# A spectral layer's row folds, made for four rows at once on one engine, with half of them made ahead of the layer

## The chip, the cores and the metric

The kernel runs on one core of one Trainium2 chip. A core has a matrix engine (TensorE; PE in the profile, with its weight loads as PEld), VectorE (DVE), ScalarE (ACT), GpSimd (POOL) and SyncE (SP), whose queue issues nearly every DMA of this kernel. All share one on-chip memory, SBUF; matmuls write to PSUM banks, from which ACT or DVE copy. The metric is the time of one execution on the device in microseconds (us); lower is better. Everything is float32 unless said otherwise.

## The reference

Four layers follow each other on a 2048 x 512 array: a spectral layer A, a state-space convolution B, A again with the same weights, B again with the same kernel. Cut to what matters:

```python
x = A_x                                            # (1, 2048, 512)
x = x + A(layernorm(x), w_r, w_i)                  # A: irfft2(rfft2(x) * (w_r + 1j * w_i))
x = x + B(layernorm(x), ...)                       # B: convolution along the rows, kernel K, plus x * D
x = x + A(layernorm(x), w_r, w_i)
x = x + B(layernorm(x), ...)

def B(u):
    C = (C_real + 1j * C_imag) * dt
    A = -exp(log_A_real) + 1j * A_imag
    K = 2 * einsum("dn,dnl->dl", C, exp(A * dt * l)).real
    return irfft(rfft(u, 4096) * rfft(K, 4096))[:2048] + u * D
```

Each layer norm is over the 512 columns of a row, without scale or shift.

## The kernel before

The 2048 rows are held as 128 partitions times 16 rows (`n2`, 0 to 15); a partition holds 16 rows of 512 columns. Every Fourier transform is a matmul with a cosine and sine matrix.

**Layer A** (`layer_a`) has three lists of steps. `spread(n2)`, L411 to L456, folds one row: with the 512 columns as four blocks of 128 (0 to 3), it makes f = blocks 0 and 1 plus blocks 2 and 3 (L443) and the difference (L444), and from these the four symmetric parts xf that a real transform needs. Part 0 is the sum of f's two blocks with the mean taken off (L447), part 1 their difference (L448), parts 2 and 3 the difference and the sum of one difference block and the other one read backwards (L449, L450), and L451 copies the one column that has no partner. In the second A layer L443, L444, L447 and L448 run on DVE and L449 to L451 on POOL (`SPL2 = 'vvggg'`). L435 on ACT scales the 128 x 128 transform matrix of that row by one over the row's deviation, four matmuls (L454) multiply the parts by it, and two ACT copies (L456) put the result into the array z. The rows are normed in groups of 2, 2, 4, 4, 4 (`GA2`) by `layer_norm_stats`, a chain of small operations: L337, L342, the square root L349 on ACT, L350, L353, L354, L355, L357, on DVE but for the root. `middle(t)` transforms the columns (`forward`, L465 to L469), multiplies by the weights, which come by DMA into `wt` tiles (L481; L483 on POOL mends two columns when they have landed; L495 is the product on DVE), and transforms back; `end(t)` folds back, adds the row and norms it.

**Layer B** (`layer_b`) goes through four blocks of 128 columns, 0 to 3. For a block `weigh` multiplies by the kernel's transform (matmul L313, products L914, sums L926 and L927 on DVE and POOL), and `back` transforms back: `units` (matmul L939, ACT copy L940) and `rows` (matmul L947, four rows at a time), in which L956 on DVE adds the layer's input `xs`, loaded by DMA (L952), and writes the sum into `h` (tile `za`), and L961 gathers the statistics for the next norm. So after block 3's four `rows` steps the second A layer has its input. The statistics of a row are whole only then; the columns of blocks 0 to 2 are final earlier.

**The order around the change.** The recording order is written out by hand (`interleave` merges lists of steps evenly). A scheduler then sets each engine's order from the recorded program by its own estimate of time, and every engine works through its own list in that order; an instruction whose wait is not over holds up what is behind it on its engine, and a DMA whose wait is not over holds up those behind it on SP. At the end of the first B layer, L1001 to L1007 record the four `rows` steps of block 3 and then all of the second A layer's `spread` steps.

**Room.** Tiles of one tag share slots in turn, and a new user waits for the readers of the old one. `t` holds B's row matrix T (2 MB), `t2` B's way back (2 MB). The transform matrix `ta` (1 MB, loaded in two pieces, L302) takes the room of `t2` and so waits for the last L947; the matrix for the way back, `in_tat`, takes it after that. Small tiles `w` share 7 slots: xs, f, xf, the scaled matrix, and the `wt` loads of the middle stage, which are tag `w` there too.

Of the kernel before, what the change touches and what calls it, by code (L numbers as in the profile page):

```python
# [19 lines left out]
RL = 4  # L20
# [12 lines left out]
LAGE = 3  # L33
# [8 lines left out]
GA2 = '22444'  # L42
# [5 lines left out]
SPL2 = 'vvggg'  # L48
# [5 lines left out]
TS2 = 'a'  # L54
# [189 lines left out]
class Net:  # L244
# [71 lines left out]
    def layer_norm_stats(self, rows, newton=False, sums=None, times=None, nr=None):  # L316
# [35 lines left out]
        for k in range(steps):  # L352
            nc.vector.scalar_tensor_tensor(t, r, -0.5, r, op0=ALU.mult, op1=ALU.mult)  # L353
            nc.vector.tensor_mul(t, t, e)  # L354
            nc.vector.scalar_tensor_tensor(nr[:, 1] if k == steps - 1 else r, t, 1.5, r, op0=ALU.add, op1=ALU.mult)  # L355
        if times is not None:
            nc.vector.tensor_scalar_mul(nr[:, 0], m, sign * times)  # L357
        else:
            nc.vector.scalar_tensor_tensor(nr[:, 0], m, -sign, nr[:, 1], op0=ALU.mult, op1=ALU.mult)
        return nr  # L360
# [18 lines left out]
    def layer_a(self, w, x=None, src=None, dst=None):  # L379
# [5 lines left out]
        spl, ya, zc, ye, we, ts = (SPL, YA, ZC, YE, WE, TS) if x is None else (SPL2, YA2, ZC2, YE2, WE2, TS2)  # L385
# [21 lines left out]
        starts = np.cumsum([0, *map(int, GA if x is None else GA2)]).tolist()  # L407
# [3 lines left out]
        def spread(n2):  # L411

            if n2 in starts:
                norm["from"] = n2
                G = starts[starts.index(n2) + 1] - n2
                norm["rows"] = [row(k_, here[k_ // 8][:, k_ % 8]) if x is None else x[:, k_] for k_ in range(n2, n2 + G)]
                if x is None and not S1:
                    norm["nr"] = self.layer_norm_stats(norm["rows"], newton=NW[0] == "1", times=-4.0)
                elif x is None:
                    norm["f"] = [self.sb("w", [2, 256]) for _ in range(G)]  # L420
                    sums = self.sb("lsum", [G], 2)
                    for k_, f in enumerate(norm["f"]):
                        r = norm["rows"][k_]
                        self.add_up(f[:, 0], r[:, 0:256], r[:, 256:512], sums[:, k_:k_ + 1])
                    norm["nr"] = self.layer_norm_stats(norm["rows"], sums=sums, times=-4.0)
                else:
                    norm["nr"] = self.layer_norm_stats([self.stats[:, n2 + k_] for k_ in range(G)], newton=NW[1] == "1", times=-4.0)
# [6 lines left out]
            if ts == "a":  # L434
                nc.scalar.activation(t, k["T"][:, n2], ACT.Copy, scale=r)  # L435
            else:
                adders[ts].tensor_scalar(t, k["T"][:, n2], r, None, op0=ALU.mult)
            x01 = split(rows[i], "abc", [2, 2, 128])
            if x is None and S1:
# [6 lines left out]
            e = [adders[c] for c in spl]  # L446
# [8 lines left out]
            for i in range(2):  # L455
                nc.scalar.copy(ZA[i][:, :, :, n2, :], p[:, :, 64 * i:64 * i + 64].rearrange("p b (q c) -> p b q c", c=4))  # L456

# [126 lines left out]
        def end(t):  # L584
            if t < 16:
                fold(t)
            if 0 <= t - LAGE < 16:
                rows_back(t - LAGE)

        return ([partial(spread, t) for t in range(16)], [partial(middle, t) for t in range(18)],  # L590
                [partial(end, t) for t in range(16 + LAGE)])
# [303 lines left out]
    def layer_b(self, kf, T, out, x=None, src=None, first=None, more=(), fill=(), switch=(), kept=None, after=None):  # L895
# [79 lines left out]
        for i, (blk, _, _, pairs) in enumerate(chain):  # L975
# [8 lines left out]
            parts = [fill[i][a:b] for a, b in zip(n, n[1:])]  # L984
            then = chain[i + 1] if i + 1 < len(chain) else (None, [], [])
# [15 lines left out]
        if after:  # L1001
            then = after()
            n = [0] * RL + list(range(0, len(then), 16 // len(last)))
            for i, f in enumerate(last):
                f()
                interleave(then[n[i]:n[i + 1]])
            last = then[n[len(last)]:]  # L1007
        interleave(last)
# [27 lines left out]
def net_kernel(ctx, tc, x, w, ends, kin, log_dt, d_skip, out, **cst):  # L1036
# [14 lines left out]
    with ExitStack() as outer:  # L1051
        with ExitStack() as early:
# [28 lines left out]
            def after():  # L1081
                wide.close()
                net.tags["wb"] = net.tags["w"]
                outer.enter_context(net.phase("x", side="right", x=(32768, 1)))
# [6 lines left out]
            wide = ExitStack()  # L1091
# [26 lines left out]
        h = net.h  # L1118
        for s in A[1:]:
# [36 lines left out]
```

## Time and profile before

| what | us |
|---|---|
| median of 3 runs (lowest, highest) | 825.46 (825.22, 829.8) |
| the profiled execution's own time | 827.06 |
| its span, first to last instruction | 825.3 |
| first B layer's last weigh sum on POOL ends | 552.65 |
| last matmuls of its way back (L947) | 558.49 to 565.90 |
| DVE: from the first L956 of block 3 to the last L448 | 560.58 to 595.96 |
| middle stage: first L465, first L495 | 598.04, 601.68 |

Engine busy time over the span is PE 82%, DVE 80%, ACT 52%, POOL 51%. These are averages over stages with different limits; what the change is worth is read from the stretch between 520 and 602 us.

### The profile page before, as it was taken

To read this page: it belongs to the slowest core of one execution; us is meant where nothing else is said; L and a number is where in the kernel's file an instruction comes from. 1 tells how busy PE (TensorE), PEld (TensorE's weight loads), DVE (VectorE), ACT (ScalarE), POOL (GpSimd) and SP (SyncE) were. 2 spreads that over 40 slices of the span, in tenths; PEclk is the share of its full clock that TensorE was granted. 3 is DMA by queue.
4 is the path that set the end of the run, shared out by engine and by line. 5 is a ranking of instruction groups with operands and counts; after the bars stand their busy time and mean duration, and the time that the engine had idled before them with its cause. 6 is when DMAs were issued, how large, how long until landed. Compare 5 with 4: busy or idle time off the path is not lost. (4 is left out here: it accounts for less than half of the span.)

```text
span 825.3 us, 13571 instructions
## 1 busy us (share of the span) xinstructions
PE 678.4 (82%) x4544; PEld 483.2 (59%) x4544; DVE 657.6 (80%) x1333; ACT 432.8 (52%) x911; POOL 419.9 (51%) x642
## 2 busy tenths in 40 slices
PE   3347889887779878799679989967799897999996
PEld 3336656664445535566356757656577673568766
DVE  7999649798998869887897868558877796977692
ACT  3525779655567855667656634213566436333212
POOL 3675876745624024822275425072855571755661
PEclk9657989999979979999989999989999999999999
DMA  8201633253566231451316557301133015323411
GB/s 323 91 1 31 148 89 107 47 136 109 140 214 178 99 44 49 90 174 35 72 33 135 185 101 209 115 1 52 54 89 89 29 27 178 102 80 100 128 49 55
DMA packets 144188, 82.24 MB, mean 100 GB/s; under 512 B 78228, under 2 KB 123928, under 8 KB 143352
## 3 DMA queue, kind: packets, MB, share of 16 engines
q1 hardware_dynamic: 143864, 80.87, 34.6%
q0 software_dynamic: 256, 0.52, 0.4%
q8 instruction: 36, 0.59, 0.3%
q14 instruction: 32, 0.26, 0.1%
HBM read 56.86 MB, written 25.03 MB: 99 GB/s over the span
## 5 line engine op out<-in xcount | busy, mean ns | idle before, releaser
L927 POOL TENSOR_TENSOR u<-wb,wb 64x512 f32<-64x512 f32 x64 | 91.9, 1436 | 121.8 <-DVE wb L914 107.1
L313 PE MATMUL p<-z,mb 128*64 128x512 f32 (+1 forms) x480 | 102.5, 542 | 6.9 <-DVE wb L914 4.5
L454 PE MATMUL p<-w,w 128*128 128x128 f32 x256 | 53.2, 369 | 51.4 <-DVE w L447 35.3
L605 ACT COPY z<-p 128x512 f32<-128x512 f32 x96 | 57.9, 615 | 70.4 <-PE p L604 60.8
L914 DVE TENSOR_TENSOR wb<-p,kk 128x512 f32<-128x512 f32 x128 | 81.3, 679 | 13.8 <-PE p L313 10.4
L827 PE MATMUL pv<-qp 128*64 128x128 f32 x1024 | 78.8, 295 | 10.4 <-DVE qp L816 8.3
L827 PEld LDWEIGHTS pv<-qp 128*64 128x64 f32 x1024 | 62.4, 146 | 40.0 <-issue 13.2
L816 DVE TENSOR_TENSOR qp<-qp,mag 128x1024 f32<-128x1024 f32 x64 | 84.9, 1331 | 0.8
L814 DVE SCALAR_TENSOR_TENSOR qp<-qp,mag 128x256 f32<-128x256 f32 x128 | 66.2, 530 | 18.7 <-ACT qp L757 18.3
L454 PEld LDWEIGHTS p<-w,w 128*128 128x128 f32 x256 | 45.1, 262 | 59.1 <-issue 25.0
L939 PE MATMUL p<-mb,u 128*128 128x128 f32 x512 | 69.0, 290 | 8.4 <-POOL u L926 6.9
L939 PEld LDWEIGHTS p<-mb,u 128*128 128x128 f32 x512 | 65.2, 203 | 16.8 <-POOL u L926 9.9
L611 DVE STREAM_TRANSPOSE z<-z 128x512 f32<-128x512 f32 x96 | 58.4, 674 | 16.5 <-ACT z L605 16.5
L940 ACT COPY u<-p 128x512 f32<-128x512 f32 x64 | 37.4, 588 | 55.7 <-PE p L939 55.6
L495 DVE TENSOR_TENSOR w<-wt,p 128x514 f32<-128x514 f32 x64 | 42.6, 687 | 30.1 <-PE p L313 20.7
L604 PE MATMUL p<-t,w 128*128 128x256 f32 x256 | 64.9, 387 | 1.0 <-POOL w L1025 0.8
L947 PEld LDWEIGHTS p<-u,t 128*128 128x128 f32 x512 | 59.1, 192 | 11.0 <-issue 5.1
L947 PE MATMUL p<-u,t 128*128 128x128 f32 x512 | 62.8, 279 | 1.4 <-ACT u L940 1.4
L313 PEld LDWEIGHTS p<-z,mb 128*64 128x64 f32 x480 | 34.0, 141 | 46.2 <-issue 24.0
L926 POOL TENSOR_TENSOR u<-wb,wb 64x512 f32<-64x512 f32 x32 | 44.6, 1394 | 22.4 <-PE p L939 17.9
L795 DVE TENSOR_SCALAR kw<-pk 128x512 bf16<-128x512 f32 x64 | 43.2, 682 | 13.4 <-PE pk L793 13.3
L604 PEld LDWEIGHTS p<-t,w 128*128 128x128 f32 x256 | 45.5, 190 | 13.6 <-issue 5.9
(189 smaller groups left out, 1552.6 us busy)
## 6 DMA issues: line engine op xcount, KB each, us to landing
wt<-in_w SPq DMA_DIRECT2D x32, 257.0 KB
w<-h SPq DMA_DIRECT2D x32, 256.0 KB
kf<-kk SPq DMA_DIRECT2D x32, 256.0 KB
kk<-kf SPq DMA_DIRECT2D x32, 256.0 KB
u<-in_x SPq DMA_DIRECT2D x16, 256.0 KB
hr<-in_x SPq DMA_DIRECT2D x16, 256.0 KB
kt<-stage SPq DMA_DIRECT2D x32, 128.0 KB
h<-hr SPq DMA_DIRECT2D x16, 256.0 KB
```

The costliest lines, as they stand in the source:

```text
L313: last = self.nc.tensor.matmul(out, weights, data, start=True, stop=True, skip_group_check=True).ins
L454: nc.tensor.matmul(p[:, b], xf[:, b], t, start=True, stop=True)
L604: nc.tensor.matmul(p[:, i], src(n2 + i), T[:, n2 + i], start=True, stop=True)
L605: nc.scalar.copy(Z[:, :, n2:n2 + 2, :].rearrange("p u n r -> p n u r"), p.rearrange("p n (u r) -> p n u r", r=2))
L611: nc.vector.transpose(tiles["zt"][:, u:u + 16].rearrange("p u d -> p (u d)"), tiles["z"][:, u:u + 16].rearrange("p u n r -> p (u n r)"))
L814: nc.vector.scalar_tensor_tensor(QP[:, c, 0], QP[:, c, 1, :, ::-1], -1.0 if c else 1.0, m[:, 0], op0=ALU.mult, op1=ALU.mult)
L816: nc.vector.tensor_mul(t, t, mag[:, None, 1:3, 256 * j:256 * j + 256].to_broadcast([128, 2, 2, 256]))
L827: nc.tensor.matmul(p[64 * t:64 * t + 64, g], QP[:, c, 2, d:d + 2].rearrange("p s a -> p (s a)"), QP[:, c, 0:2, d:d + 2].rearrange("p k s b ...
L914: nc.vector.tensor_mul(split(m[c, pl], "du", [16, 32]), by_channel(p), split(k[c], "du", [16, 32]))
L927: e[1].tensor_add(y[64:128], v[0, 1], v[1, 0])
L939: nc.tensor.matmul(p[:, i], Y[:, d + i], MBT, start=True, stop=True)
L947: nc.tensor.matmul(p[:, i], TBT[:, n0 + i, r], V[:, n0 + i, r].rearrange("p q d -> p (q d)"), start=r == 0, stop=r == 1)
```

## The change

Only the second A layer's first stage and its neighbours are touched.

- The even blocks' folds, block 0 plus block 2 and block 0 minus block 2, are made in eight DVE operations of four rows each while block 3 is still to be done (block 2's columns are final by then). They are kept in a tile `even` of 16,384 bytes per partition, in T's room, whose last reader in this layer was the forward transform of block 3.
- `spread_four(n0)` takes the place of `spread` there: four rows at once on DVE, in operations of 512 columns. L468 makes blocks 1 minus 3, L464 blocks 1 plus 3, L466 part 0 for one row (four of them), L467 part 1, L469 and L470 parts 2 and 3. Two small ACT copies (L471, L472) take POOL's column copy. POOL has no part in it. L464 is tied behind the norm's last operation (`issue_after`).
- Norm groups are 4, 4, 4, 4.
- The recording order becomes: rows 0, rows 1, spread 0, rows 2, spread 1, rows 3, spread 2, spread 3.
- The transform matrix, `fa` and `xf` get their own room (phase `folds`), which the first B layer's weigh products had. So the matrix, now tile `tb`, no longer waits for L947.
- T's room is taken, so T is loaded once more (2 MB) when the folds are done.

```diff
-        spl, ya, zc, ye, we, ts = (SPL, YA, ZC, YE, WE, TS) if x is None else (SPL2, YA2, ZC2, YE2, WE2, TS2)
+        ya, zc, ye, we = (YA, ZC, YE, WE) if x is None else (YA2, ZC2, YE2, WE2)
...
+        def spread_four(n0):
+
+            if n0 == 0:
+                k["T"] = self.load("tb", "ta", [16, 128], cut=512)
+            nr = self.layer_norm_stats([self.stats[:, n0 + i] for i in range(4)], newton=NW[1] == "1", times=-4.0)
+            ns = np.s_[:, n0:n0 + 4]
+            g = [self.even[:, i, n0:n0 + 4] for i in range(2)]
+            a, b = (x[:, n0:n0 + 4, 128 * c:128 * c + 128] for c in (1, 3))
+            f = self.sb("fa", [2, 4, 128])
+            xf = self.sb("xf", [4, 4, 128])
+            with self.tc.issue_after(self.normed):
+                nc.vector.tensor_add(f[:, 0], a, b)
+            for i in range(4):
+                nc.vector.scalar_tensor_tensor(xf[:, 0, i], g[0][:, i], nr[:, 0, i:i + 1], f[:, 0, i], op0=ALU.add, op1=ALU.add)
+            nc.vector.tensor_sub(xf[:, 1], g[0], f[:, 0])
+            nc.vector.tensor_sub(f[:, 1], a, b)
+            nc.vector.tensor_sub(xf[:, 2, :, 1:], g[1][:, :, 1:], f[:, 1, :, 127:0:-1])
+            nc.vector.tensor_add(xf[:, 3, :, 1:], g[1][:, :, 1:], f[:, 1, :, 127:0:-1])
+            nc.scalar.copy(xf[:, 2, :, 0], g[1][:, :, 0])
+            nc.scalar.copy(xf[:, 3, :, 0], f[:, 1, :, 0])
+            for i in range(4):
+                t = self.sb("w", [128])
+                nc.scalar.activation(t, k["T"][:, n0 + i], ACT.Copy, scale=nr[:, 1, i:i + 1])
+                p = self.ps("p1", [4, 128])
+                for c in range(4):
+                    nc.tensor.matmul(p[:, c], xf[:, c, i], t, start=True, stop=True)
+                for j in range(2):
+                    nc.scalar.copy(ZA[j][:, :, :, n0 + i, :], p[:, :, 64 * j:64 * j + 64].rearrange("p b (q c) -> p b q c", c=4))
...
+            if more and i == len(chain) - 1:
+
+                self.even = self.sb("t", [2, 16, 128])
+                parts[2] = parts[2] + [partial(op, self.even[:, c, n0:n0 + 4], self.h[:, n0:n0 + 4, 0:128], self.h[:, n0:n0 + 4, 256:384])
+                                       for c, op in enumerate((nc.vector.tensor_add, nc.vector.tensor_sub)) for n0 in range(0, 16, 4)]
...
             then = after()
-            n = [0] * RL + list(range(0, len(then), 16 // len(last)))
-            for i, f in enumerate(last):
-                f()
-                interleave(then[n[i]:n[i + 1]])
-            last = then[n[len(last)]:]
-        interleave(last)
+            last = [*last[:1], *[f for pair in zip(last[1:], then) for f in pair], *then[len(last) - 1:]]
+        for f in last:
+            f()
...
-                outer.enter_context(net.phase("x", side="right", x=(32768, 1)))
+                folds.enter_context(net.phase("folds", side="right", tb=(8192, 1), fa=(4096, 2), xf=(8192, 2)))
...
         h = net.h
+        folds.close()
+        outer.enter_context(net.phase("x", side="right", x=(32768, 1)))
+        T = net.load("t", "t", [16, 256])
```

The built programs' orders, at the places that the prediction speaks of. In the rows of the program after, L980 is L956 of before, L985 is L961, L915 is L891, L976 is L952, L298 is L302, L505 is L481, and the norm's L333, L338, L346, L349 to L351 and L353 are L337, L342, L350, L353 to L355 and L357.

DVE, at the end of the first B layer's block 2, before (`p` is the matmul's PSUM tile, `w` is xs):

```order
L956 TENSOR_TENSOR za_4668<-w_4931,p_1182_4922 128x4x128
L961 BN_STATS stats_66<-za_4668 128x6 x4
L956 TENSOR_TENSOR za_4668<-w_4964,p_1188_4955 128x4x128
L961 BN_STATS stats_66<-za_4668 128x6 x4
L956 TENSOR_TENSOR za_4668<-w_4980,p_1190_4971 128x4x128
L961 BN_STATS stats_66<-za_4668 128x6 x4
L956 TENSOR_TENSOR za_4668<-w_5008,p_1196_4999 128x4x128
L961 BN_STATS stats_66<-za_4668 128x6 x4
L887 TENSOR_SCALAR kf_1_65<-kk_5016,kc_2604 64x16
```

The same place after; `t_5047` is the tile `even`:

```order
L980 TENSOR_TENSOR za_4668<-w_4931,p_1182_4922 128x4x128
L985 BN_STATS stats_66<-za_4668 128x6 x4
L228 TENSOR_TENSOR t_5047<-za_4668 128x512 x2
L980 TENSOR_TENSOR za_4668<-w_4964,p_1188_4955 128x4x128
L980 TENSOR_TENSOR za_4668<-w_4980,p_1190_4971 128x4x128
L985 BN_STATS stats_66<-za_4668 128x6 x4
L228 TENSOR_TENSOR t_5047<-za_4668 128x512 x2
L985 BN_STATS stats_66<-za_4668 128x6 x4
L228 TENSOR_TENSOR t_5047<-za_4668 128x512 x2
L980 TENSOR_TENSOR za_4668<-w_5008,p_1196_4999 128x4x128
L985 BN_STATS stats_66<-za_4668 128x6 x4
L228 TENSOR_TENSOR t_5047<-za_4668 128x512 x2
```

The eight even folds stand among block 2's sums, ahead of block 3's weigh products (the next L914 in before).

DVE, in the spread, before: two rows of the middle of it.

```order
L443 TENSOR_TENSOR w_5289<-za_4668 128x256
L444 TENSOR_TENSOR w_5289<-za_4668 128x256
L353 SCALAR_TENSOR_TENSOR lnt_5363<-lnr_5362 128x4
L350 RECIPROCAL lnr_5450<-lnt_5451 128x4
L447 SCALAR_TENSOR_TENSOR w_5292<-w_5289,lnn_5252 128x128
L448 TENSOR_TENSOR w_5292<-w_5289 128x128
```

After, from the first group's fold to block 3's third `rows` sum:

```order
L464 TENSOR_TENSOR fa_5248<-za_4668 128x512
L353 TENSOR_SCALAR lnn_5313<-bmv_5314 128x4
L346 RECIPROCAL lnr_5320<-lnt_5321 128x4
L468 TENSOR_TENSOR fa_5329<-za_4668 128x512
L466 SCALAR_TENSOR_TENSOR xf_5249<-t_5047,lnn_5232,fa_5248 128x128 x4
L467 TENSOR_TENSOR xf_5249<-t_5047,fa_5248 128x512
L349 SCALAR_TENSOR_TENSOR lnt_5321<-lnr_5320 128x4
L469 TENSOR_TENSOR xf_5330<-t_5047,fa_5329 128x4x127
L470 TENSOR_TENSOR xf_5330<-t_5047,fa_5329 128x4x127
L350 TENSOR_TENSOR lnt_5321<-lnt_5321,lnv_5319 128x4
L980 TENSOR_TENSOR za_4668<-w_5306,p_1266_5297 128x4x128
```

Five 512-wide operations and four 128-wide ones now stand for four rows, in place of four sets of L443, L444, L447 and L448; the third and fourth `rows` sums of block 3 come between the groups instead of ahead of them all.

SP, the DMA queue around the spread, before (`ta_5266` the transform matrix, `ta_6229` the one of the way back):

```order
L891 DMA kf<-kk_5033 128x512
L302 DMA ta_5266<-in_ta 128x512
L302 DMA ta_5266<-in_ta 128x1536
L302 DMA ta_6229<-in_tat 128x2048
L481 DMA wt_5631<-in_w 128x514
L481 DMA wt_5646<-in_w 128x514
```

All loads of xs (L952) stand ahead of this piece. After:

```order
L915 DMA kf<-kk_5016 128x512
L298 DMA tb_5229<-in_ta 128x512
L298 DMA tb_5229<-in_ta 128x1536
L298 DMA ta_6140<-in_tat 128x2048
L976 DMA w_5306<-h_63 128x4x128
L976 DMA w_5387<-h_63 128x4x128
L298 DMA t_5528<-in_t 128x4096
L505 DMA wt_5542<-in_w 128x514
L505 DMA wt_5557<-in_w 128x514
```

The xs loads of block 3's third and fourth `rows` steps now stand behind the two matrices, and T's 2 MB stand ahead of the first weights of the middle stage. On POOL the 48 operations of L449 to L451 are gone, on PE and ACT only the spread's own rows and copies differ, and past the first L495 the orders of all engines are the same as before.

More of the change, by code (lines that the diff above doesn't have):

```diff
@@ L19 @@
 NW = '000'
-RL = 4
 POS = 3
@@ L41 @@
 XNE = 'gggg'
-GA2 = '22444'
 GA = '22444'
@@ L47 @@
 YE = 'g'
-SPL2 = 'vvggg'
 TS = 'a'
@@ L53 @@
 WE2 = 'g'
-TS2 = 'a'
 MAG = 4
@@ L354, in layer_norm_stats @@
             nc.vector.tensor_mul(t, t, e)
-            nc.vector.scalar_tensor_tensor(nr[:, 1] if k == steps - 1 else r, t, 1.5, r, op0=ALU.add, op1=ALU.mult)
+            last = nc.vector.scalar_tensor_tensor(nr[:, 1] if k == steps - 1 else r, t, 1.5, r, op0=ALU.add, op1=ALU.mult).ins
         if times is not None:
@@ L359, in layer_norm_stats @@
             nc.vector.scalar_tensor_tensor(nr[:, 0], m, -sign, nr[:, 1], op0=ALU.mult, op1=ALU.mult)
+        self.normed = last
         return nr
@@ L405, in row @@
             return t
-        starts = np.cumsum([0, *map(int, GA if x is None else GA2)]).tolist()
+        starts = np.cumsum([0, *map(int, GA)]).tolist()
         norm = {}
@@ L415, in spread @@
                 G = starts[starts.index(n2) + 1] - n2
-                norm["rows"] = [row(k_, here[k_ // 8][:, k_ % 8]) if x is None else x[:, k_] for k_ in range(n2, n2 + G)]
-                if x is None and not S1:
+                norm["rows"] = [row(k_, here[k_ // 8][:, k_ % 8]) for k_ in range(n2, n2 + G)]
+                if not S1:
                     norm["nr"] = self.layer_norm_stats(norm["rows"], newton=NW[0] == "1", times=-4.0)
-                elif x is None:
+                else:
                     norm["f"] = [self.sb("w", [2, 256]) for _ in range(G)]
@@ L425, in spread @@
                     norm["nr"] = self.layer_norm_stats(norm["rows"], sums=sums, times=-4.0)
-                else:
-                    norm["nr"] = self.layer_norm_stats([self.stats[:, n2 + k_] for k_ in range(G)], newton=NW[1] == "1", times=-4.0)
             i = n2 - norm["from"]
@@ L433, in spread @@
             r = nr[:, 1, i:i + 1]
-            if ts == "a":
+            if TS == "a":
                 nc.scalar.activation(t, k["T"][:, n2], ACT.Copy, scale=r)
             else:
-                adders[ts].tensor_scalar(t, k["T"][:, n2], r, None, op0=ALU.mult)
+                adders[TS].tensor_scalar(t, k["T"][:, n2], r, None, op0=ALU.mult)
             x01 = split(rows[i], "abc", [2, 2, 128])
-            if x is None and S1:
+            if S1:
                 f = norm["f"][i].rearrange("p i (a b) -> p i a b", b=128)
@@ L445, in spread @@
             xf = self.sb("w", [4, 128])
-            e = [adders[c] for c in spl]
+            e = [adders[c] for c in SPL]
             nc.vector.scalar_tensor_tensor(xf[:, 0], f[:, 0, 0], nr[:, 0, i:i + 1], f[:, 0, 1], op0=ALU.add, op1=ALU.add)
@@ L588, in end @@
                 rows_back(t - LAGE)
-        return ([partial(spread, t) for t in range(16)], [partial(middle, t) for t in range(18)],
-                [partial(end, t) for t in range(16 + LAGE)])
+        return ([partial(spread, t) for t in range(16)] if x is None else [partial(spread_four, t) for t in range(0, 16, 4)],
+                [partial(middle, t) for t in range(18)], [partial(end, t) for t in range(16 + LAGE)])
     def forward_b(self, src, T, tag="z"):
@@ L1090, in net_kernel @@
             at = cuts[1]
-            wide = ExitStack()
+            wide, folds = ExitStack(), ExitStack()
             def switch():
```

## The prediction

> **What bounds the kernel now.** I read the page's busy line first, and then left averages for stretches of the layers' seam: the windows view gives, for each, its length and then the busy time and instruction count of PE, PEld, DVE, ACT and POOL, the granted clock, the DMA share and GB/s.
>
> ```profile
> PE 678.4 (82%) x4544; PEld 483.2 (59%) x4544; DVE 657.6 (80%) x1333; ACT 432.8 (52%) x911; POOL 419.9 (51%) x642
> ```
> ```profile
> 521.04:533.24 12.20, 12.20 (x87) 9.03 (x87) 6.86 (x23) 3.51 (x6) 0.00 (x0) 1.00 0.34 125
> 547.21:560.58 13.37, 11.54 (x76) 11.35 (x77) 1.65 (x2) 5.57 (x9) 5.23 (x4) 0.74 0.00 0
> 560.58:595.96 35.38, 25.13 (x167) 21.45 (x166) 35.34 (x130) 14.65 (x49) 21.87 (x48) 0.95 0.12 36
> 595.96:601.68 5.72, 4.32 (x36) 3.48 (x34) 0.00 (x1) 3.52 (x11) 1.43 (x7) 1.00 0.63 248
> 601.68:652.89 51.21, 47.50 (x365) 35.98 (x361) 41.31 (x80) 30.40 (x90) 28.51 (x74) 1.00 0.27 73
> 690.50:697.50 7.00, 5.07 (x15) 2.27 (x16) 3.64 (x23) 6.65 (x13) 0.00 (x0) 1.00 0.89 336
> ```
>
> From 560.58 to 595.96 DVE is busy 35.34 of 35.38 us: the last `rows` sums of the first B layer and the second A layer's folds are bound by DVE alone, though over the span PE is the busiest engine. Behind it, PE fills 47.50 of 51.21 us. So what the fold stage gains or loses at the first product L495 (601.68) should reach the end nearly whole. DVE has room ahead: 1.65 us of work between 547.21 and 560.58, and it idles 5.34 of the 12.20 us between 521.04 and 533.24.
>
> The timeline shows one row of the steady spread, and its end (start, length, engine, line, operation, in brackets the idle time before it and who ended it).
>
> ```profile
> 592.12 0.34 DVE L447 SCALAR_TENSOR_TENSOR w<-w,lnn 128x128 f32<-128x128 f32 x1
> 592.30 1.16 PE L454 MATMUL p<-w,w 128*128 128x128 f32 x8 [0.50 <-POOL w L451]
> 592.38 0.28 DVE L448 TENSOR_TENSOR w<-w 128x128 f32<-128x128 f32 x1
> 592.58 0.67 DVE L443 TENSOR_TENSOR w<-za 128x256 f32<-128x256 f32 x1
> 593.17 0.67 DVE L444 TENSOR_TENSOR w<-za 128x256 f32<-128x256 f32 x1
> 593.77 0.34 DVE L447 SCALAR_TENSOR_TENSOR w<-w,lnn 128x128 f32<-128x128 f32 x1
> ...
> 598.04 0.49 PE L465 MATMUL p<-ca,z 128*128 128x132 f32 x2 [0.46 <-ACT z L456]
> ...
> 601.68 1.29 DVE L495 TENSOR_TENSOR w<-wt,p 128x514 f32<-128x514 f32 x2 [5.72 <-PE p L313]
> ```
>
> A row takes DVE 1.65 us (592.12 to 593.77), start to start .26 for L447, .20 for L448, .59 for L443, .60 for L444. PE then waits for POOL's L451 in each row, but POOL's chain starts from DVE's L444, so it only trails it.
>
> **The change: DVE's work.** The two halves of a row cost this much because of a neighbour.
>
> ```profile
> L443 DVE TENSOR_TENSOR w<-za x16: 360/671/674, 568.6 to 594.2; 128x256 f32<-128x256 f32 x16
> ```
> ```profile
> 568.57 0.36 DVE L443 TENSOR_TENSOR w<-za 128x256 f32<-128x256 f32 x1
> 568.85 0.41 DVE L444 TENSOR_TENSOR w<-za 128x256 f32<-128x256 f32 x1
> ```
> ```profile
> L676 DVE TENSOR_TENSOR tmp<-tmp 128x512 f32<-128x512 f32 x1 | 0.7, 669 | 0.0
> ```
> ```profile
> L448 POOL TENSOR_TENSOR w<-w 128x128 f32<-128x128 f32 x16 | 9.6, 599 | 21.5 <-DVE w L443 19.4 <-PE p L454 1.9
> L450 POOL TENSOR_TENSOR w<-w 128x127 f32<-128x127 f32 x32 | 18.4, 574 | 0.0
> ```
>
> L443's shortest run is 360 ns, the first one, when POOL had nothing to do; the median, with POOL's folds beside it, is 671. A 512-wide operation (L676) takes 669 ns with nothing beside it. So DVE spends in the steady spread on 256 columns what it spends alone on 512. Less the .07 us by which operations overlap (L443 lasts .67, L444 starts .59 later), I price a 512-wide fold at .60, and half of the spread's price was POOL's neighbourhood, which the change takes away.
>
> The Trainium skill, "Perfetto Trace Analysis", Optimizing Scalar/DVE Operations, says that when DVE is saturated, offloading work to GPSIMD may make sense, which speaks against this change, and adds that the two share an SBUF read port, so that it might not help. By the first half alone the stage would get longer, with DVE already full; the 360 against 671 ns stand with the second half.
>
> Parts 2 and 3 (L469, L470) read one operand backwards, which DVE does nowhere in this trace. On POOL a reversed 127-wide operation (L450, 574 ns) is no slower than a straight 128-wide one (599). I take .60 for DVE too; the other bound is the doubled price, 1.26 (671/360 of .669), and there is no reason for less than .60.
>
> The norms and sums stay; their steps are these.
>
> ```profile
> 560.58 0.69 DVE L956 TENSOR_TENSOR za<-w,p 128x512 f32<-128x512 f32 x1 [11.72 <-PE p L947]
> 561.30 0.87 DVE L961 BATCH_NORM_STATS2 stats<-za 128x6 f32<-128x128 f32 x4
> 562.09 0.61 DVE L337 BATCH_NORM_AGGREGATE bmv<-stats 128x2 f32<-128x24 f32 x4
> 562.62 0.63 DVE L956 TENSOR_TENSOR za<-w,p 128x512 f32<-128x512 f32 x1
> 563.16 0.16 DVE L342 TENSOR_SCALAR lnv<-bmv 128x2 f32<-128x2 f32 x1
> 563.23 0.16 DVE L357 TENSOR_SCALAR lnn<-bmv 128x2 f32<-128x2 f32 x1
> ```
>
> A sum takes .72, four statistics .79, four aggregates .53, a small norm operation about .075. A group of four rows then costs DVE 5 x .60 (L464, L467 to L470) + 4 x .26 (L466, the form of L447) + .72 + .79 + .53 + 6 x .075 = 6.53 us, four groups 26.1. From 560.58 that ends at 586.7; I add .8 for results needed at once by the next operation: 587.5. The same sum for before, 16 x 1.65 + 4 x 2.04 + some 26 x .075 = 36.6, is 1.2 above the true 35.38, so it isn't short.
>
> **The even folds** are eight operations, 4.8 us, in an earlier stage.
>
> ```profile
> 521.04 0.69 DVE L956 TENSOR_TENSOR za<-w,p 128x512 f32<-128x512 f32 x1 [0.72 <-PE p L947]
> ...
> 528.46 0.69 DVE L956 TENSOR_TENSOR za<-w,p 128x512 f32<-128x512 f32 x1 [2.26 <-PE p L947]
> ...
> 533.24 1.29 DVE L914 TENSOR_TENSOR wb<-p,kk 128x512 f32<-128x512 f32 x2 [1.47 <-PE p L313]
> ```
>
> The idle time of 5.34 us there is 12.20 less 6.86, with POOL at 0.00, so that no doubled price is due. Laid into the order shown, they are through at about 532.8, .4 ahead of the first weigh product. Cover: PE, full in that stretch. If it fails, what is behind L914 shifts one for one; bounds 0 and about 1, I take 0. The small copies L471 and L472 go to ACT, busy 14.65 of 35.38 us: nothing.
>
> **The transform matrix and the queue.** Before, its load waited for the last L947; now for POOL's last weigh sum.
>
> ```profile
> 551.39 1.26 POOL L926 TENSOR_TENSOR u<-wb,wb 64x512 f32<-64x512 f32 x1
> ```
> ```profile
> 569.25 0.69 ACT L435 ACTIVATE w<-ta,lnn 128x128 f32<-128x128 f32 x2 [1.66 <-DMA ta<-in_ta]
> ```
> ```profile
> 558.49 7.41 PE L947 MATMUL p<-u,t 128*128 128x128 f32 x64 [0.68 <-ACT u L940]
> ```
>
> It issues at 552.65 and, at the 336 GB/s of a full queue (690.50 to 697.50), has landed by 558, long ahead of ACT's need. That takes away 1.66 us on an engine that wasn't the bound: nothing by itself. The next on SP, `in_tat`, waits for the last L947 (565.90) and holds up the xs loads of rows 2 and 3; the first lands at about 571.0 (1 MB at 336 GB/s is 3.1 us, and some 2 us of latency and xs), when DVE wants it at about 571.2. I take 0, with 2 us as the other bound. At the end T, 2 MB, issues at 587.5 and stands ahead of the two `wt` loads.
>
> ```profile
> 594.01 0.33 SPq L302 DMA_DIRECT2D ta<-in_tat  x1
> 595.57 1.10 SPq L481 DMA_DIRECT2D wt<-in_w  x2
> 599.80 0.19 POOL L483 COPY wt<-ends 128x4 f32<-128x4 f32 x1 [2.69 <-DMA wt<-in_w]
> ```
>
> 2.36 MB at 336 GB/s are 7.0 us. To that comes what lies around a transfer: in before 1.3 MB, 3.9 us at that rate, took 5.8 from `in_tat`'s issue (594.01) to L483 (599.80), a part of it the wait of the `wt` issue itself. With .9 to 1.9 us for it the first `wt` is ready at 595.4 to 596.4.
>
> **The tail.** In before PE trails DVE by a row. In after PE can't begin a row of the last group until L467, its last fold, is done. 64 matmul records took 7.41 us (L947, above), a row's eight .93: four rows 3.7 and ACT's last copy .46, so the forward transform starts at 591.7 instead of 598.04: 6.3 us earlier, and L495 (3.64 later, as before) at 595.3, level with `wt` or up to 1.1 ahead of it. From this goes a clock loss, which the windows of before show elsewhere.
>
> ```profile
> 564.69:568.10 3.41, 1.21 (x11) 1.02 (x10) 3.41 (x21) 0.20 (x1) 0.00 (x0) 1.00 0.33 94
> 568.10:571.51 3.41, 1.56 (x8) 1.25 (x8) 3.41 (x17) 1.08 (x4) 1.75 (x4) 0.95 0.53 216
> 571.51:574.93 3.42, 3.42 (x17) 3.11 (x16) 3.42 (x13) 1.67 (x6) 2.24 (x7) 0.55 0.00 0
> ```
>
> Two stretches with PE under half busy are followed by one at half clock. In after PE runs in bursts, one per group, and by my laying-out idles from about 579.5 to 582 or 583.5; the half clock then falls at about 585 to 589, over the tail's beginning and the third group's leftovers. Bounds 0 and 3.7 (all four rows at half pace); I take 1.5, which puts L495 at 596.8 and covers `wt`. The Trainium skill, "TensorE: Matmul & The Clock Gate", What's actually happening, has the clock halved after one idle window of about 3.4 us; by that, with stretches of pure idleness under 3.4 us, there would be no loss here, while the rows show it after stretches a third busy.
>
> Sum: 6.3 - 1.5 = 4.8 us. The profiled execution's 827.06 (span 825.3) would become 822.3 (820.5); on the median of 825.46, which lies 1.6 lower, 820.7.
>
> **The rivals.**
> - *No clock loss, and DVE no slower than priced.* For it: half clock depends on where the windows fall. 825.46 - 6.3 = 819.2, or 820.3 where `wt` comes at 596.4; if the .8 and some of the prices are too high as well (T then goes out earlier too), down to 816.5. Only below 817.2 is it over 1%.
> - *Transfers take the place of DVE.* xs behind `in_tat` (2 us) or T ahead of `wt` (at the 248 GB/s of the window from 595.96, 9.5 us, so L483 at about 597.9 and L495 at 598) become the bound. For it: both are level with DVE in my sum. 822.5 to 824.5, middle 823.5.
> - *DVE's wide operations cost more than .60: slower.* The place is L469 and L470, eight operations on the path. At 1.26 each they add 5.3, and the time is 826.0; it decides from 1.2 us each (8 x .6 = 4.8 eats the gain). Were all twenty wide operations at 1.26, 13.2 less 4.8 makes 833.9. Against it: the POOL rows and the idle POOL.
> - *The gain is made and eaten later*, PE having a wait on something unmoved, say the T reload's traffic in the middle stage: 825. Against it: PE's 47.50 of 51.21 us.
>
> **How the numbers follow.** My forecast (819.5 to 822.5) has 0.55, the first rival 0.20, transfers 0.12, wide operations 0.08, the eaten gain 0.05. The range 816.5 to 825.6 holds all but the slower case and the first rival's last edge. A measurement of this kernel tells about 1% from no change, 8.3 us. Faster than 817.2: two fifths of the first rival, 0.08. Slower than 833.7: the worst of the wide operations, 0.03. Within: 0.89.
>
> **What would show it.** Right: L464, L467 to L470 at about 670 ns; the reversed ones as the straight ones; DVE full from the first sum (at about 560.6) to the last L467 near 587.5; first forward matmul at 591 to 594; a half-clock stretch near 585 to 589; the first L914 of block 3 still at about 533.2. Wrong: reversed folds of 1 us or more; DVE waiting for xs by DMA; POOL's mending copy, by DMA, last ahead of L495; no clock loss; or the stretch from L495 to the end longer than before's 223.6 (825.3 - 601.68).

## The result: 0.7% faster, and where the time went

The changed kernel takes 821.91 us (median of 14 runs, 818.59 to 824.53), the kernel before, beside it, 827.0 us (823.51 to 835.14): a ratio of 0.9929, 95% interval 0.9907 to 0.9951. Measured once more, 12 runs beside 29 of before, it was 0.9965 (0.9938 to 0.9992). By the medians that is 5.1 and 3.5 us; 4.8 were forecast (820.7 us from the then median of 825.46).

The profiled execution of the kernel after took 821.88 us, its span is 820.1. The windows of its stretches (length; busy time and count of PE, PEld, DVE, ACT, POOL; granted clock, DMA share, GB/s; in the rows of the kernel after, L519 is L495 of before, L507 is L483, L478 is L454, L480 is L456, L489 is L465, L475 is L435 and L971 is L947):

```profile
519.89:532.09 12.20, 12.20 (x87) 9.03 (x87) 11.16 (x31) 3.52 (x6) 0.00 (x0) 1.00 0.26 100
546.11:559.49 13.38, 11.62 (x76) 11.43 (x77) 1.58 (x1) 4.39 (x9) 5.16 (x4) 0.74 0.22 78
559.49:586.21 26.72, 17.82 (x139) 16.13 (x138) 26.18 (x96) 14.33 (x50) 0.19 (x2) 1.00 0.18 60
586.21:595.85 9.64, 8.33 (x69) 7.44 (x68) 0.01 (x2) 6.25 (x19) 0.39 (x3) 1.00 0.73 272
595.85:649.82 53.97, 49.42 (x369) 37.46 (x369) 40.23 (x81) 30.14 (x89) 28.70 (x75) 1.00 0.27 70
```

DVE's stretch from block 3's first sum to its last fold is 26.72 us instead of 35.38, and DVE is still full in it. Behind it stands a gap that is longer than before: 9.64 us from the last fold to the first product, against 5.72. Its timeline:

```profile
559.49 0.69 DVE L980 TENSOR_TENSOR za<-w,p 128x512 f32<-128x512 f32 x1 [11.80 <-PE p L971]
...
562.68 0.68 DVE L469 TENSOR_TENSOR xf<-t,fa 128x508 f32<-128x508 f32 x1
563.27 0.68 DVE L470 TENSOR_TENSOR xf<-t,fa 128x508 f32<-128x508 f32 x1
563.86 0.17 DVE L338 TENSOR_SCALAR lnv<-bmv 128x4 f32<-128x4 f32 x1
...
570.55 0.69 DVE L980 TENSOR_TENSOR za<-w,p 128x512 f32<-128x512 f32 x1 [0.29 <-DMA w<-h]
...
584.48 1.14 DVE L466 SCALAR_TENSOR_TENSOR xf<-t,lnn,fa 128x128 f32<-128x128 f32 x4
585.53 0.68 DVE L467 TENSOR_TENSOR xf<-t,fa 128x512 f32<-128x512 f32 x1
595.85 1.29 DVE L519 TENSOR_TENSOR w<-wt,p 128x514 f32<-128x514 f32 x2 [9.63 <-POOL wt L507]
```

And what lies between those last two rows, on ACT, PE, SP and POOL:

```profile
583.20 0.65 ACT L480 COPY z<-p 128x256 f32<-128x256 f32 x2 [2.36 <-PE p L478]
583.93 1.28 ACT L475 ACTIVATE w<-tb,lnn 128x128 f32<-128x128 f32 x4
585.12 1.16 ACT L480 COPY z<-p 128x256 f32<-128x256 f32 x4
```
```profile
582.23 2.83 PE L478 MATMUL p<-w,xf 128*128 128x128 f32 x20 [0.58 <-DVE xf L467]
585.79 4.95 PE L478 MATMUL p<-w,xf 128*128 128x128 f32 x40 [0.73 <-ACT z L480]
591.20 0.49 PE L489 MATMUL p<-ca,z 128*128 128x132 f32 x2 [0.46 <-ACT z L480]
```
```profile
586.28 0.34 SPq L298 DMA_DIRECT2D t<-in_t  x1
586.75 13.99 SPq L505 DMA_DIRECT2D wt<-in_w  x4
```
```profile
595.62 0.19 POOL L507 COPY wt<-ends 128x4 f32<-128x4 f32 x1 [8.31 <-issue]
596.23 0.19 POOL L507 COPY wt<-ends 128x4 f32<-128x4 f32 x1 [0.41 <-DMA wt<-in_w]
```

The first forward matmul comes at 591.20, 31.71 us after block 3's first sum (37.46 before, 5.75 less); the first product L519 at 595.85, 36.36 after it (41.10 before, 4.74 less). What ends the wait for the product is now POOL's mending copy of the weights, 9.34 us after T's issue, and not PE. The profile names a DMA as what the second such copy waited for; for the first it says "issue", that is, nothing that it shows. That the first one too waited for its weights is taken from the runs with T behind weights, below: there this wait for POOL is gone.

The spans differ by 5.2 us. 4.74 of that is gained between block 3's first sum and the first product. Another 1.09 lies ahead: block 3's first sum stands at 559.49 instead of 560.58, and block 2's, ahead of every changed instruction, already at 519.89 instead of 521.04; that is scatter between two executions. The remaining .6 are lost behind the first product (224.25 us to the end against 223.6), also within scatter: between first and last product, identical code took 47.7 us here and 46.4 in a second profiled execution of the same kernel (rows below). The last window above ends at the first operation behind the products (L574, L550 of before); the like stretch of before ends at 654.83 and lasts 53.15 us, 2 more than the window from 601.68 to 652.89 that the prediction shows. For this reason the experiments are read by stretches that begin at block 3's first sum, and the whole times only for what they can tell, about 2 us either way.

### The profile page after: what moved, and what is told of

The parts are those of the page before. It is cut to its first block, busy times and chain, and to the rows that moved or that the text cites. A ratio compares the mean times of both kernels' runs of the same rounds, so it can differ in the third digit from the quotient of the medians.

```text
span 820.1 us, 13475 instructions
## 1 busy us (share of the span) xinstructions
PE 675.2 (82%) x4544; PEld 481.8 (59%) x4544; DVE 653.4 (80%) x1307; ACT 433.4 (53%) x918; POOL 396.4 (48%) x594
## 5 line engine op out<-in xcount | busy, mean ns | idle before, releaser
L938 DVE TENSOR_TENSOR wb<-p,kk 128x512 f32<-128x512 f32 x128 | 81.3, 679 | 13.1 <-PE p L309 9.6
L519 DVE TENSOR_TENSOR w<-wt,p 128x514 f32<-128x514 f32 x64 | 42.5, 686 | 33.3 <-PE p L309 13.8
L971 PEld LDWEIGHTS p<-u,t 128*128 128x128 f32 x512 | 59.1, 192 | 11.1 <-issue 5.9
L449 PE MATMUL p<-w,w 128*128 128x128 f32 x128 | 31.9, 427 | 40.3 <-DVE w L442 37.9
L971 PE MATMUL p<-u,t 128*128 128x128 f32 x512 | 62.8, 278 | 1.4 <-ACT u L964 1.4
L449 PEld LDWEIGHTS p<-w,w 128*128 128x128 f32 x128 | 27.7, 318 | 44.3 <-issue 25.3
```

The source lines that it names most:

```text
L449: nc.tensor.matmul(p[:, b], xf[:, b], t, start=True, stop=True)
L938: nc.vector.tensor_mul(split(m[c, pl], "du", [16, 32]), by_channel(p), split(k[c], "du", [16, 32]))
L971: nc.tensor.matmul(p[:, i], TBT[:, n0 + i, r], V[:, n0 + i, r].rearrange("p q d -> p (q d)"), start=r == 0, stop=r == 1)
```

## Experiments

All stretches in us from block 3's first sum, read from each timeline.

| kernel | last DVE fold ends | first forward matmul | first product | ratio to before (95%) |
|---|---|---|---|---|
| before | 35.38 | 37.46 | 41.10 | |
| after | 26.72 | 31.71 | 36.36 | 0.9929 (0.9907, 0.9951) |
| all folds on DVE, else as before | 35.39 | 36.62 | 40.26 | 1.0012 (0.9982, 1.0042) |
| even folds late | 31.37 | 36.15 | 39.91 | 0.9993 (0.9967, 1.0020) |
| parts 2, 3 on POOL | 28.12 | 35.14 | 38.90 | 1.0001 (0.9973, 1.0029) |
| T behind six weights | 27.26 | 32.62 | 36.38 | 0.9961 (0.9935, 0.9986) |
| T behind all weights | 26.78 | 31.76 | 35.52 | 0.9949 (0.9917, 0.9981) |
| the same, part 1 first | 27.01 | 32.00 | 35.76 | 0.9970 (0.9937, 1.0004) |
| after, again | 26.70 | 31.69 | 36.26 | 0.9965 (0.9938, 0.9992) |
| matrix late | 27.06 | 32.44 | 36.89 | 0.9970 (0.9941, 1.0000) |
| T last, ACT reordered | 26.96 | 31.76 | 35.52 | 0.9968 (0.9942, 0.9994) |

**All folds on DVE, nothing else.** The price in question: whether POOL's neighbourhood doubled L443 and L444.

```diff
-SPL2 = 'vvggg'
+SPL2 = 'vvvvv'
```

> The kernel before with all folds of the second layer on DVE: L449, L450 and L451 leave POOL, nothing else is changed. Stretch from the first sum of block 3 (first L956) to the first forward matmul: 37.46 us in before. Theory (POOL beside it doubled the price of L443 and L444): L443 and L444 fall from 671 to about 360 ns, a row costs DVE .28 + .28 + .26 + .20 + 2 x .20 + .08 = 1.50 instead of 1.65 though DVE does more, and the stretch is about 34.5, 3 us shorter; time about 3 us below before (ratio 0.996). Rival (671 ns is what 256 columns cost, POOL or not): a row costs 1.65 + .48 = 2.13, the stretch is some 8 us longer, ratio 1.009.

The line's own view (shortest, median, longest ns), and the window of the stretch to the first forward matmul:

```profile
L443 DVE TENSOR_TENSOR w<-za x16: 361/412/417, 570.5 to 595.7; 128x256 f32<-128x256 f32 x16
```
```profile
562.50:599.12 36.62, 26.25 (x176) 23.09 (x175) 35.36 (x178) 15.82 (x53) 0.39 (x4) 0.91 0.15 53
```

L443 falls from 671 to 412 ns with POOL idle (.39 us in the stretch, 21.87 in a like stretch before). DVE executes 48 instructions more (178 against 130) and is busy 35.36 us, as long as before (35.34). The rival's 8 us more did not come: the neighbourhood was real. But the 3 us less didn't come either: I had priced the undisturbed 256-wide operation by its first run, 360 ns; the median is 412. What leaving POOL saves, POOL's work uses up. Taking POOL out is thus no gain by itself at DVE's end; it is what makes the move to DVE free.

**Even folds back in the spread.** One part undone.

```diff
-                parts[2] = parts[2] + [partial(op, self.even[:, c, n0:n0 + 4], ...) ...]
...
             with self.tc.issue_after(self.normed):
+                nc.vector.tensor_add(g[0], x[:, n0:n0 + 4, 0:128], x[:, n0:n0 + 4, 256:384])
+                nc.vector.tensor_sub(g[1], x[:, n0:n0 + 4, 0:128], x[:, n0:n0 + 4, 256:384])
                 nc.vector.tensor_add(f[:, 0], a, b)
```

> The changed kernel with the even folds put back into the spread: two 512-wide DVE operations more per group, tied behind the group's norm, none during block 2. Theory (the eight folds stood in DVE's waits and cost nothing there): eight times .60 come back on the path, the stretch from block 3's first sum to the first forward matmul grows from 31.71 to about 36.5, close to the 37.46 of before; ratio to before 0.998 to 0.999. Rival (the gain is the idle POOL and the four-row operations, the early folds only fill other waits of the spread): the stretch grows by less than 2.5 us, ratio 0.995 or less.

Its timeline (L982 is the sum, L469 part 1, L491 the forward matmul here):

```profile
555.98 0.69 DVE L982 TENSOR_TENSOR za<-w,p 128x512 f32<-128x512 f32 x1 [11.62 <-PE p L973]
...
586.67 0.68 DVE L469 TENSOR_TENSOR xf<-t,fa 128x512 f32<-128x512 f32 x1
```
```profile
592.13 0.49 PE L491 MATMUL p<-ca,z 128*128 128x132 f32 x2 [0.46 <-ACT z L482]
```

The forward transform starts 36.15 us after the first sum, 4.44 later than in the changed kernel, near the 4.8 that were priced, and the time is that of before. This kernel has everything of the change but the early folds. With the run above it splits DVE's 8.66 us: all folds on DVE, nothing (35.38 to 35.39); four rows at once, together with the column copies on ACT, the new norm groups and order and the early matrix, 4.02 (to 31.37); even folds early, 4.65 (to 26.72). At the first forward matmul the same steps are .84, .47 and 4.44. The step to four rows gains hardly anything there: from the last fold to the forward transform it is 4.78 us with it (4.99 in the changed kernel), and 1.23 in the row-by-row run. A likely reason is that PE can finish no row of a group before the fold over all four rows is done; no run undoes that alone.

One reservation: PE ran the third group here at half clock (granted .53 from 580.90 to 587.35), which the changed kernel didn't. DVE was busy 30.92 of its 31.37 us, so its own 4.65 owe little to that; what part of the 4.44 at PE does can't be told from this profile.

**Parts 2 and 3 on POOL.** The contention from the other side.

```diff
-            nc.vector.tensor_sub(xf[:, 2, :, 1:], ...)
-            nc.vector.tensor_add(xf[:, 3, :, 1:], ...)
+            nc.gpsimd.tensor_sub(xf[:, 2, :, 1:], ...)
+            nc.gpsimd.tensor_add(xf[:, 3, :, 1:], ...)
```

> The changed kernel with parts 2 and 3 (L469, L470) on POOL instead of DVE: 4.8 us less DVE work. Theory (shared port): POOL takes about 2 us for each, 16 us in the spread, and the other wide DVE operations rise from 680 ns towards 1.3 us where they overlap; the stretch from block 3's first sum to the first forward matmul is 1 to 3 us longer than 31.71. Rival (no contention of this size): DVE is relieved and the stretch is 2 to 4 us shorter.

The last group's folds on DVE and POOL:

```profile
581.44 0.68 DVE L467 TENSOR_TENSOR xf<-t,fa 128x512 f32<-128x512 f32 x1
582.04 1.23 DVE L349 SCALAR_TENSOR_TENSOR lnt<-lnr 128x4 f32<-128x4 f32 x1
583.31 1.19 DVE L350 TENSOR_TENSOR lnt<-lnt,lnv 128x4 f32<-128x4 f32 x1
584.53 0.16 DVE L351 SCALAR_TENSOR_TENSOR lnn<-lnt,lnr 128x4 f32<-128x4 f32 x1
```
```profile
581.51 1.74 POOL L469 TENSOR_TENSOR xf<-t,fa 128x508 f32<-128x508 f32 x1 [4.30 <-PE p L478]
583.22 1.26 POOL L470 TENSOR_TENSOR xf<-t,fa 128x508 f32<-128x508 f32 x1
```

Relieved of eight wide operations (4.8 us), DVE ends 1.40 us later than in the changed kernel, and the forward transform comes 3.43 later, a little beyond the theory's 1 to 3. DVE was busy 26.79 us for 88 instructions, against 26.18 for 96 in the changed kernel: what it was relieved of came back in longer operations. Of the 3.43, the other 2.03 lie behind the last fold, where PE had half the clock (granted .62 from 586.40 to 590.90), so the forward transform overstates the contention. The manner was not as I had it. The wide folds keep their 680 ns; it is small operations of the norm, four columns wide, that last 1.23 and 1.19 us instead of about .16: each ends when POOL's operation ends (583.25, 584.48). And POOL's L469 lasts 1.74 instead of 1.26 where it begins during DVE's L467. In these rows each engine waits for the other's operation to end.

**T behind the sixth weight load.** What ends the wait for the first product (`net.fetched` is the latest weight DMA).

```diff
-        T = net.load("t", "t", [16, 256])
-        for s in A[1:]:
+        T = []
...
+        def again():
...
+            with tc.issue_after(net.fetched):
+                T.append(net.load("t", "t", [16, 256]))
...
+        for s in [[*A[1][:6], again, *A[1][6:]], *A[2:]]:
             interleave(s)
+        T = T[0]
```

> The changed kernel with T's reload put behind the sixth weight load instead of ahead of the first. Theory (T ahead of the weights sets the first product): the first product L519 comes 3.64 us after the first forward matmul as in before, not 4.65, and the two later waits for weights (.76 and 1.08 us) go: 1.0 to 2.5 us less than the changed kernel, ratio to before about 0.991. Rival (the 2 MB only move the wait to later weights, or PE would have been late anyway): the same time as the changed kernel, ratio 0.993, with weights waited for behind the sixth.

```profile
597.32 1.29 DVE L519 TENSOR_TENSOR w<-wt,p 128x514 f32<-128x514 f32 x2 [9.12 <-PE p L309]
...
612.61 0.69 DVE L519 TENSOR_TENSOR w<-wt,p 128x514 f32<-128x514 f32 x1 [1.00 <-POOL wt L507]
...
618.18 1.29 DVE L519 TENSOR_TENSOR w<-wt,p 128x514 f32<-128x514 f32 x2 [1.58 <-POOL wt L507]
```

Both were half right. PE now ends the wait, 3.76 us after the first forward matmul instead of 4.65; but the weights behind T are waited for, 1.00 and 1.58 us, and the products take longer from first to last than in any other run (below). The 2 MB moved the wait.

This run also shows the half clock that the prediction charged, and where it had put it, about 24 to 28 us after the first sum. Its fold code is that of the changed kernel, but the forward transform stands at 32.62 instead of 31.71:

```profile
584.20:586.00 1.80, 1.78 (x12) 1.78 (x13) 1.73 (x6) 0.72 (x3) 0.00 (x0) 0.77 0.00 0
586.00:588.00 2.00, 2.00 (x11) 1.94 (x11) 1.96 (x6) 1.73 (x6) 0.19 (x2) 0.50 0.00 0
```

Not all of these .91 us belong to it. DVE's last fold ends .54 later already (27.26 against 26.72): .23 of that is a longer wait for xs (.51 us against .29), the rest follows a wait of DVE for ACT's square root, which here stands behind copies that waited for PE; PE had half the clock in the second group too, and that this was the cause is not shown by itself. What is left behind the last fold is .37 (5.36 against 4.99).

**T behind all weights**, and **the changed kernel again**, side by side. The first differs from the run above in one line:

```diff
-        for s in [[*A[1][:6], again, *A[1][6:]], *A[2:]]:
+        for s in [[*A[1], again], *A[2:]]:
```

> The changed kernel with T's reload put behind all sixteen weight loads, where the DMA engines are idle (about 640 to 665 us). Theory (the 2 MB cost what they hold up, wherever weights stand behind them): the first product comes 3.6 to 3.8 us after the first forward matmul (4.65 in the changed kernel), and the stretch from it to the first L574 is 53.2 or less (53.97; 55.21 with T behind the sixth weight), so some 1.5 us less than the changed kernel measured beside it. Rival (those differences are scatter between executions, not T): the stretch stays at 54 or above and the time the same.

> The changed kernel once more, beside the other two. Theory: as measured, ratio to before 0.993, and first product 4.65 us after the first forward matmul, ended by the weights, or later where the tail is free of the half clock; with a half-clock stretch in the tail the first forward matmul stands at some 32.6 us after block 3's first sum instead of 31.7 and the weights are in time. Rival (a single profile misled, the weights are rarely last): the product is ended by PE at 3.64 with no half clock in the tail.

The first product with T last, and in the changed kernel again:

```profile
594.18 1.29 DVE L519 TENSOR_TENSOR w<-wt,p 128x514 f32<-128x514 f32 x2 [8.74 <-PE p L309]
```
```profile
597.58 1.29 DVE L519 TENSOR_TENSOR w<-wt,p 128x514 f32<-128x514 f32 x2 [9.55 <-POOL wt L507]
```

First and last start of all 32 products, in the changed kernel, the same again, T behind six weights, and T last:

```profile
L519 DVE TENSOR_TENSOR w<-wt,p x32: 681/688/692, 595.8 to 643.5; 128x514 f32<-128x514 f32 x32
```
```profile
L519 DVE TENSOR_TENSOR w<-wt,p x32: 682/688/693, 597.6 to 644.0; 128x514 f32<-128x514 f32 x32
```
```profile
L519 DVE TENSOR_TENSOR w<-wt,p x32: 681/688/692, 597.3 to 646.2; 128x514 f32<-128x514 f32 x32
```
```profile
L519 DVE TENSOR_TENSOR w<-wt,p x32: 682/688/692, 594.2 to 641.0; 128x514 f32<-128x514 f32 x32
```

The changed kernel repeats itself in the spread: 31.69 (31.71) to the forward transform, 4.57 (4.65) from there to the product, ended by the weights. So T ahead of the weights costs .8 to .9 us between the forward transform and the first product (3.76 with T behind weights), and .7 to .8 at the first product (35.52 with T last). Beyond that nothing is settled: from first to last product it is, in the order of the rows, 47.7, 46.4, 48.9 and 46.85 us. Only T behind six is outside what the two executions of the changed kernel do. The stretch to the first L574 was 54.67 with T last, not the 53.2 that I expected, and 54.38 in the changed kernel again; both had a half-clock stretch between the last product and that operation, which the profiles of the changed kernel's first measurement and of T behind six had not. As whole times, 0.9949 (0.9917 to 0.9981) against 0.9965 (0.9938 to 0.9992): T last may be the best of all these kernels, but the intervals lie over each other.

**Part 1 ahead of part 0**, with T last: the order of two fold steps.

```diff
                 nc.vector.tensor_add(f[:, 0], a, b)
+                nc.vector.tensor_sub(xf[:, 1], g[0], f[:, 0])
             for i in range(4):
                 nc.vector.scalar_tensor_tensor(xf[:, 0, i], ...)
-            nc.vector.tensor_sub(xf[:, 1], g[0], f[:, 0])
```

> As the run with T last, and part 1 (xf[:, 1], L467) recorded ahead of the four part-0 operations (L466), so that the last group's first row is whole after the first L466, not after all of it. Theory (the tail begins with DVE's last operation of a row): the first forward matmul comes .5 to 1.0 us earlier after block 3's first sum than in the run with T last, where neither has a half-clock stretch in the tail. Rival (PE is still busy with the third group's rows then): less than .3 us.

**ACT's order at the groups' border**, with T last (`copied` is the last copy of the third row of the group before):

```diff
                 t = self.sb("w", [128])
-                nc.scalar.activation(t, k["T"][:, n0 + i], ACT.Copy, scale=nr[:, 1, i:i + 1])
+                with ExitStack() as stack:
+                    if "copied" in k:
+                        stack.enter_context(self.tc.issue_after(k["copied"]))
+                    nc.scalar.activation(t, k["T"][:, n0 + i], ACT.Copy, scale=nr[:, 1, i:i + 1])
...
```

> As the run with T last, and on ACT the four scaled matrices of a group (L475) stand behind the copies (L480) of the third row of the group before, not ahead of the second row's. Theory (at the end of the spread ACT waits for the last group's norm while two rows of the third group lie uncopied, so that PE begins the third group's last row only at 26.3 us after block 3's first sum and the tail is five rows long, not four): the first forward matmul comes .5 to 1.0 us earlier than 31.7, and the first product with it, at 34.5 to 35.0. Rival (the tail is set by DVE's last fold alone): within .3 us of 31.7.

Both tried to shorten the tail, and both failed: 32.00 and 31.76 to the forward transform, against 31.76 with T last alone. PE at the end of the spread, part 1 first (L467 is part 0 there), and then with ACT reordered (L481, L483 and L495 are L478, L480 and L489):

```profile
581.27 3.02 PE L478 MATMUL p<-w,xf 128*128 128x128 f32 x24 [2.19 <-DVE xf L467]
585.40 4.95 PE L478 MATMUL p<-w,xf 128*128 128x128 f32 x40 [1.11 <-ACT z L480]
590.81 0.49 PE L489 MATMUL p<-ca,z 128*128 128x132 f32 x2 [0.46 <-ACT z L480]
```
```profile
584.17 5.02 PE L481 MATMUL p<-w,xf 128*128 128x128 f32 x36 [0.58 <-DVE xf L467]
589.44 3.05 PE L481 MATMUL p<-w,xf 128*128 128x128 f32 x24 [0.24 <-ACT z L483]
592.95 0.49 PE L495 MATMUL p<-ca,z 128*128 128x132 f32 x2 [0.46 <-ACT z L483]
```

In all three forms PE has the rows of the last two groups to do from the moment that the third group is folded, and needs 8.8 to 9.5 us until the forward transform: 582.23 to 591.20 in the changed kernel, 581.27 to 590.81 and 584.17 to 592.95 here. That the tail hangs on DVE's last fold alone, or on ACT's order alone, does not fit these. That it is the pace of eight rows through PE fits all of them: in the changed kernel ACT's copies of the last five rows start .9 to 1.0 us apart (586.99 to 590.77), each after a wait for PE. It wasn't tested by itself.

**The transform matrix late again.** The room undone.

```diff
-                k["T"] = self.load("tb", "ta", [16, 128], cut=512)
+                k["T"] = self.load("ta", "ta", [16, 128], cut=512)
```

> The changed kernel with the transform matrix back in the room of t2, so that its load waits for the last L971 again and the matrix of the way back comes after the spread. Theory (the early matrix is worth nothing by itself, DVE bounds the spread): first forward matmul 31.7 us after block 3's first sum as before, within .5; but the queue then holds 1 MB more ahead of the weights, so the first product comes some 3 us later, 7 to 8 us after the first forward matmul instead of 4.6, and the time is about 3 us above the changed kernel, ratio 0.998. Rival (PE's first group is delayed by 2 us and the buffers of folds carry that to DVE): the first forward matmul is 1.5 us or more later.

```profile
568.35 4.53 PE L478 MATMUL p<-w,xf 128*128 128x128 f32 x24 [3.87 <-ACT w L475]
...
591.60 0.49 PE L489 MATMUL p<-ca,z 128*128 128x132 f32 x2 [0.46 <-ACT z L480]
```
```profile
585.20:586.70 1.50, 1.50 (x8) 1.40 (x8) 1.03 (x3) 1.19 (x5) 0.00 (x0) 0.52 0.53 82
588.20:589.70 1.50, 1.50 (x15) 1.50 (x15) 0.00 (x0) 1.07 (x4) 0.00 (x0) 1.00 1.19 497
```

PE's first group does wait for the matrix, but the forward transform is only .73 later. Of that .34 stands at the last fold already (27.06 against 26.72): DVE waited .63 us for xs here instead of .29. The other .39 lies behind the last fold, with a half-clock stretch there (first window) at the same place as in the run with T behind six weights, where it was .37. So the early matrix is worth some .3 us in the spread at most. The second half of my expectation fell: 1 MB more ahead of the weights made the first product .5 us later, not 3. The DMA engines moved 497 GB/s in the second window; I had priced 336.

## Why the prediction was right, step by step

- **DVE in the spread**, 26.9 us from the first sum to the last fold: measured 26.72 and 26.70. The wide operations start .59 to .60 after each other (562.68, 563.27, 563.86), and the reversed L469 takes no longer than the straight L464 (the groups of the kernel after), so the rival that priced it at 1.26 and ended slower is out.

```profile
L464 DVE TENSOR_TENSOR fa<-za 128x512 f32<-128x512 f32 x4 | 2.7, 684 | 0.0
L469 DVE TENSOR_TENSOR xf<-t,fa 128x508 f32<-128x508 f32 x4 | 2.7, 676 | 0.0
```

- **The doubled price beside POOL** held as a mechanism (671 to 412 ns), not in its size (360): it is 1.6 times, not 1.9. The sum did not use that number; it was used to argue where the gain comes from, and there I saw too much in it: leaving POOL and taking over its work cancel, and it is the early even folds that carry most of the change.
- **The even folds at nothing.** Right (L938 is L914 of before): from block 2's first sum to block 3's first product it is 12.20 us before and after, while DVE's busy time in it went from 6.86 to 11.16 us. Laying-out and chip agree here within the .4 us that I gave as spare: .74 remain.

```profile
531.12 0.23 DVE L913 TENSOR_SCALAR kk<-kk,kc 64x16 f32<-64x16 f32 x1
532.09 1.89 DVE L938 TENSOR_TENSOR wb<-p,kk 128x512 f32<-128x512 f32 x3 [0.74 <-PE p L309]
```

- **xs behind the matrix.** Taken at 0; .29 us of waiting at 570.55, none for the fourth step.
- **The tail**, four rows and a copy, 4.2 us behind the last fold: 4.99. The step that failed is "PE can't begin a row of the last group until L467, its last fold, is done" as the thing that sets the end: forty matmul records, five rows, run from 585.79, .4 ahead of the end of L467, since the third group's last row was still to be done. The price of a row was good (.93 forecast, .9 to 1.0 between ACT's copies); the number of rows was one short.
- **The clock loss**, 1.5 us: 0 in both profiled executions of the changed kernel, whose granted clock is 1.00 all through the spread. In the runs with T behind six weights and with the late matrix, where it fell as forecast over the third group's leftovers and the tail's beginning, .37 and .39 lie behind the last fold. It exists, but not each time; as a fixed term it was too large. The Trainium skill's "TensorE: Matmul & The Clock Gate", What's actually happening, gave no loss here by the prediction's reading, since PE's gaps stay under 3.4 us. For the changed kernel's two profiles that was right. For the clock other runs disagree with that reading: with T behind all weights it was halved in the first group (568.90 to 572.30, granted .53, and the forward transform is no later than in the changed kernel), with T behind six in the second group and the tail, each time after gaps of 2.9 us at most.

```profile
568.90:572.30 3.40, 3.02 (x16) 2.72 (x14) 3.07 (x10) 2.39 (x9) 0.00 (x0) 0.53 0.28 77
```

- **Weights behind T**, ready at 34.8 to 35.8 us after the first sum, level with PE: 36.1, and they were last. T's issue to the first mended weights took 9.34 us, where I had laid out 7.9 to 8.9.

The sum came out at 4.8 for a gain of 4.74 at the first product, and that closeness is luck: 1.5 us of clock loss weren't there and DVE was .2 earlier, against .8 more in the tail and 1.0 that the product waited for weights. The main term, DVE's folds, was right in its mechanism and its size. The forecast's likeliest case said that the clock loss covers the weights; what happened is nearer to its rival of transfers in DVE's place, whose range of 822.5 to 824.5 doesn't follow from its own figure for T: L495 at 598 is 3.7 us earlier than before, so 821.8. Of the signs that the prediction named as wrong, three came: no clock loss, POOL's mending copy last ahead of the product, and DVE waiting for xs by DMA, though only .29 us. Another, a longer stretch from the product to the end, came by .6 us, which scatter covers. Behind the first product the gain went through to the end as far as the scatter lets one see.

## What to carry to other kernels

When an engine bounds a stage, look for work of that stage whose inputs are final earlier, and lay it into the engine's waits in the stage before: here that was most of the gain, 4.44 of 5.75 us at the next stage's start, while the step to fewer and wider instructions moved DVE's end by 4 us and the next stage's start by half of one, probably because PE then gets its work in lumps. A tile that takes another's room brings that one's reload, and the reload stands in a queue: behind the weights it made the first product .7 to .8 us earlier, though the whole times don't tell the two places apart. Where a neighbour raises an engine's price, taking over the neighbour's work need not gain anything: here DVE's busy time was the same with and without it.

## What was not expected of the hardware

An operation of DVE that meets one of POOL can last until that one ends, however small it is itself: 1.19 us for a norm operation on four columns that takes .16 elsewhere, beside a POOL operation of 1.26. In one case POOL waits for DVE in the same way (1.74 for 1.26). Reading backwards costs DVE nothing (676 ns for 508 columns against 684 for 512). And the half clock falls differently on the same fold code from one execution to the next: nowhere in the spread in both profiles of the changed kernel, in the first group with T behind all weights, and in the second group and the tail with T behind six. Of the nine profiles with four-row folds, six show a half-clock stretch in the spread.
